# Four attention steps of batches 2 and 3 issued beside the channel mixing of batches 0 and 1, with x allotted at the first product with v

## The chip, the cores and the metric

The kernel runs on one core of one Trainium2 chip. The metric is the device time of an execution in microseconds (us). The profile is one execution of the same program, with its own time.

## What is computed

Three blocks follow each other, for 4 batches of 576 positions with 8 heads of 64 (d_model 512), all in float32. Cut to what matters:

```python
# attention, per batch and head; heads 0-3 see the last 32 positions, heads 4-7 every 4th of the last 128
scores = where(mask, q @ k.T / sqrt(64), -1e9)
x = softmax(scores) @ v                      # heads side by side: (4, 576, 512)
# first mixing block
theta = x @ w_theta
y = w_tok_r @ (x * cos(theta)) + w_tok_i @ (x * sin(theta))   # over positions
u = x + y
x = u + relu(u @ w_ch)                       # over channels
# second block
h = relu(x @ w_in); u, v = halves(h)
out = (u * (w_spatial @ layernorm(v) + b_spatial)) @ w_out
```

## The kernel before

Every float32 product of the mixing blocks is made of three products of rounded parts: a high and a low part of each operand (names ending in _h and _l, zh and zl, uh and ul), high by high, low by high, high by low. The parts are made by `split`: the high part by a cast on ACT, DVE or POOL, the low part by a subtraction on POOL.

The work of a batch b has four stages. `attention(b)` is a generator of 16 steps over 12 groups of rows (four pairs of heads, three groups in each). At a step, `att_values` of the group four steps back, `att_transpose` of the group two steps back and `att_scores` of a new group are issued. Scores are six small products into the PSUM tile s; then, for the batches from 1 on, DVE adds the mask (sm), takes the maximum (m), ACT makes three exponentials with their sums (l), DVE adds a small number and inverts l, and POOL multiplies sm by it. att_transpose turns sm on PE (pt) and copies it to pT. att_values multiplies pT with v (ps_x) and ACT copies the product into x, the batch's activations.

`th_run(b)` runs units of the theta stage, one for each 128 positions: DVE splits x into xh and xl, PE makes ps_th, ACT and DVE reduce it to an angle (ta, tb), ACT takes sine and cosine, PE turns x (ps_xn), DVE multiplies, and the result is split into zh and zl: unit t gives tiles t (cosine) and 4+t (sine), tile 8 holds the last 64 positions of both. `tm_run(b)` mixes positions: 8 units, each one PSUM sum ps_y over all z tiles (27 products with tile 8, 24 without), added to x, then split into uh and ul. `ch_run(b)` mixes channels: 8 units of 12 products (ps_r), added to x, split into a tile "parts" and stored by SP in x2d.

The weights of the second block are split while the first block runs, in 32 jobs (`second`): SP loads a piece, POOL or ACT and DVE turn its 64-bit form into w64g (or it comes as `stage`), a cast and a POOL subtraction fill a tile parts, SP stores it. `parts` has two buffers, which these jobs and the channel mixing share. The PSUM pool ps_mm has four banks, for s, ps_th, ps_y and ps_r. x has two buffers.

`spread(main, (fill, rate), ...)` issues a main generator and, after each of its steps, so many steps of the fills. Batch 0's attention and theta stage come first. Then for b = 0 and 1: tm_run(b) and four units of ch_run(b), with attention(b+1) spread in at two steps a unit; th_run(b+1); and the last four units of ch_run(b). After that come tm_run(2) with attention(3) at three steps a unit (and, chained behind it, one theta unit that batches 2 and 3 share, from the tile xs), then th_run(3) with the rest of batch 2. The second block follows.

That is the order in which the program is issued. A scheduler then places the instructions in one in-order queue for each engine: earlier issued work comes first, and later work goes ahead of it where the scheduler's own times say that the earlier isn't ready. All DMAs go through SP's queue. The text calls the stretch between th_run(1) and tm_run(1) seam A, the same between batches 1 and 2 seam B, and the end of attention(3) with the following xs the tail.

Of the kernel before, what the change touches and what calls it, by code (L numbers as in the profile page):

```python
# [11 lines left out]
F32 = mybir.dt.float32  # L12
# [11 lines left out]
P = 128  # L24
# [19 lines left out]
ATT_RATE, ATT_RATE_PAIR = 2.0, 3.0  # L44
TAIL_RATE = 1.0
CH_BEFORE = 4
PE_MASK = 1
PAIR = 2

# [12 lines left out]
def tile_block(ctx: ExitStack, tc: tile.TileContext, qT, kT, vw, eye_in, mask_in, eye_b_in, w_theta, w_tok, w_ch, w_in, w_sp, w_sph, b_sp, w_out, out):  # L62
# [106 lines left out]
    x = {}  # L169
# [30 lines left out]
    def att_scores(m):  # L200

        b, hp, g = groups[m]
        if g == 0:
            att_load(b, hp)
        if hp == 0 and g == 0:
            x[b] = p1.tile([P, 4, S], F32, tag="x", name=f"x{b}", bufs=2)
        qz, kt, vt, pT = heads[b, hp]
        s = ps_mm.tile([P, 512], F32, tag="mm", name="s")
        kind = 2 * (hp // 2) + g // 2
# [41 lines left out]
    def att_values(m):  # L251

        b, hp, g = groups[m]
        if g == 0:
            return
        qz, kt, vt, pT = heads[b, hp]
        ps = ps_t.tile([P, 512], F32, tag="pt", name="ps_x")
        if g == 1:
            for t in range(NA):
                for j in range(2):  # L260
                    PE.matmul(ps[T * j:T * (j + 1), T * t:T * (t + 1)], vt[:, t, T * j:T * (j + 1)], pT[j][:, T * t:T * (t + 1)], start=True, stop=True)
        else:
            for t in range(NB):
                for j in range(2):
                    PE.matmul(ps[T * j:T * (j + 1), T * t:T * (t + 1)], vt[:, NA + t, T * j:T * (j + 1)], pT[2][:, P * t + T * j:P * t + T * (j + 1)], start=True, stop=True)
        n0, n1 = (0, NA * T) if g == 1 else (NA * T, S)
        if hp < 2:
            A.copy(x[b][:, hp, n0:n1], ps[:, :n1 - n0])
            return

        xv = x[b][:, hp, :].rearrange("p (i r) -> p r i", r=4)
        if g == 1:
            A.copy(xv[:, :2, :], ps[:, :2 * SEQ].rearrange("p (r i) -> p r i", r=2))
            A.copy(xv[:, 2, :NA * T - 2 * SEQ], ps[:, 2 * SEQ:NA * T])
        else:
            A.copy(xv[:, 2, NA * T - 2 * SEQ:], ps[:, :3 * SEQ - NA * T])
            A.copy(xv[:, 3, :], ps[:, 3 * SEQ - NA * T:NB * T])
# [81 lines left out]
    def th_run(b, ts):  # L359
        for t in ts:  # L360
            th_unit(b, t)
            yield
# [46 lines left out]
    def spread(main, *fills):  # L409

        acc = [0.0] * len(fills)
        for _ in main:
            for i, (gen, rate) in enumerate(fills):
                acc[i] += rate
                while acc[i] >= 1.0:
                    acc[i] -= 1.0
                    next(gen, None)
        for gen, _ in fills:
            run(gen)

    def jobs(fns):
        for f in fns:
            f()
            yield

    def take(gen, n):
        for _ in range(n):
            yield next(gen)

    def chain(*gens):  # L430
        for g in gens:
            yield from g
# [11 lines left out]
    second = jobs(j_in + j_sp + j_out)  # L444
    spread(attention(0), (jobs(j_theta + j_tok0), W_RATE0))
    spread(th_run(0, (4, 0, 1, 2, 3)), (jobs(j_tok1), 1.0))
    for b in range(PAIR):
        ch = ch_run(b)
        spread(chain(tm_run(b, K_ALL), take(ch, CH_BEFORE)), (attention(b + 1), ATT_RATE), (take(second, 12) if b else jobs(j_ch), 1.0 if b else 0.5))
        run(th_run(b + 1, (4, 0, 1, 2, 3) if b + 1 < PAIR else (0, 1, 2, 3)))  # L450
        run(ch)


    th_keep(PAIR)
    spread(tm_run(PAIR, K_MAIN, False), (chain(attention(PAIR + 1), th_shared(PAIR)), ATT_RATE_PAIR), (take(second, 10), 1.25))
    spread(th_run(PAIR + 1, (0, 1, 2, 3)), (chain(tm_run(PAIR, (8,)), ch_run(PAIR)), TAIL_RATE), (second, 2.5))
    patt.release()
    ps_v.release()
# [294 lines left out]
```

## Time and profile before

| | before |
|---|---|
| time, three runs | 575.29, 578.91 and 1181.34 us, median 578.91 |
| the profiled execution's own time | 575.99 us |
| its span | 574.2 us |
| mean granted PE clock | 0.973 |
| PE busy | 538.3 us, 94% of the span |
| DVE, POOL, ACT busy | 329.7, 259.6, 243.3 us |

The span is the time between the first and the last record of the profile, which lies within the execution's own time. The granted clock is a share of the full 2.4 GHz. A busy share is a mean over the whole span, and stages differ.

### The profile page before, as it was taken

How to read it: one execution, taken by the hardware profiler on the slowest of the kernel's cores; microseconds unless marked ns; L12 is line 12 of the kernel's file. 1: busy time of each engine (PE TensorE's matmuls, PEld its weight loads, DVE VectorE, ACT ScalarE, POOL GpSimd, SP SyncE). 2: the span in 40 equal slices, each digit the busy share in tenths (PEclk: the TensorE clock that was granted, in tenths of full speed). 3: DMA queues.
4: the chain of work that ended last, by engine and by line, in shares of the span. 5: the costliest groups of instructions: out<-in, count | busy, mean ns of one | idle time of the engine just before them, and what ended most of it. 6: DMA issues, size and time to landing. Idle time of an engine off the chain costs nothing.

```text
span 574.2 us, 11260 instructions
## 1 busy us (share of the span) xinstructions
PE 538.3 (94%) x4148; PEld 479.7 (84%) x4148; DVE 329.7 (57%) x842; ACT 243.3 (42%) x712; POOL 259.6 (45%) x329
## 2 busy tenths in 40 slices
PE   4958889999999999999799999999999999999997
PEld 2745668888988798888688999899889989988996
DVE  3767999965888548956688215773620227354030
ACT  3765475644465624677365111442332223233222
POOL 2755577633696436955339633343211303432040
PEclk9877989999999999999799999999999999999999
DMA  8996224762157644486510699805024120001002
GB/s 226 232 254 176 75 88 113 208 190 83 43 158 231 180 121 153 144 261 211 186 31 1 217 374 373 287 13 166 0 75 132 52 74 1 0 2 57 18 1 92
DMA packets 49935, 76.07 MB, mean 132 GB/s; under 512 B 4052, under 2 KB 30552, under 8 KB 49880
## 3 DMA queue, kind: packets, MB, share of 16 engines
q1 hardware_dynamic: 49880, 75.35, 42.9%
q8 instruction: 33, 0.54, 0.4%
q14 instruction: 22, 0.18, 0.1%
HBM read 52.53 MB, written 22.81 MB: 131 GB/s over the span
## 4 chain that ended last, share of the span: by engine, by line
PE 60%; DVE 13%; DMA 12%; POOL 5%; issue 4%; ACT 3%; SPq 1%; POOLq 0%; ACTq 0%; DVEq 0%
PE ps_y L377 10%; PE ps_sp L628 9%; PE ps_hu L609 9%; PE ps_o L657 9%; PE ps_hv L564 9%; PE ps_r L395 6%; DMA w<-w_tok 3%; PE s L220 2%; DMA w<-w_in 2%; DMA wsp_d<-parts 2%; PE ps_th L322 2%; POOL zl L297 2%; PE pt L247 1%; DMA qz<-qT 1%; DMA w<-w_ch 1%
## 5 line engine op out<-in xcount | busy, mean ns | idle before, releaser
L377 PE MATMUL ps_y<-wtok_h,zh 128*128 128x288 f32 x288 | 87.1, 308 | 3.3 <-DVE sm L231 1.3
L377 PE MATMUL ps_y<-wtok_h,zl 128*128 128x288 f32 x288 | 86.8, 303 | 2.4 <-POOL zl L297 2.4
L377 PE MATMUL ps_y<-wtok_l,zh 128*128 128x288 f32 x288 | 85.3, 297 | 0.0
L377 PEld LDWEIGHTS ps_y<-wtok_h,zh 128*128 128x128 f32 x288 | 53.9, 190 | 7.3 <-DVE sm L231 2.0
L297 POOL TENSOR_TENSOR gl<-hu,gh 128x288 fp32r<-128x288 f32 x32 | 26.0, 813 | 74.4 <-ACT gh L108 74.4
L377 PEld LDWEIGHTS ps_y<-wtok_h,zl 128*128 128x128 f32 x288 | 54.8, 190 | 4.4 <-POOL zl L297 3.2
L377 PEld LDWEIGHTS ps_y<-wtok_l,zh 128*128 128x128 f32 x288 | 54.7, 190 | 0.0
L632 DVE TENSOR_TENSOR hu<-ps_sp,hu 128x288 f32<-128x288 f32 x32 | 14.6, 456 | 67.0 <-PE ps_sp L631 66.9
L297 POOL TENSOR_TENSOR vl<-hv,vh 128x512 fp32r<-128x512 f32 x16 | 20.9, 1309 | 62.7 <-ACT vh L108 57.6
L235 ACT ACTIVATE sm<-sm,m 128x96 f32<-128x96 f32 x108 | 39.2, 364 | 14.6 <-DVE m L232 13.2
L220 PE MATMUL s<-kt,qz 128*64 128x96 f32 x576 | 42.3, 270 | 1.3 <-DMA qz<-qT 0.5
L220 PEld LDWEIGHTS s<-kt,qz 128*64 128x64 f32 x576 | 31.2, 147 | 11.1 <-issue 6.4
L238 POOL TENSOR_TENSOR sm<-sm,l 128x288 f32<-128x288 f32 x48 | 32.1, 673 | 18.1 <-DVE l L237 15.1
L297 POOL TENSOR_TENSOR ul<-x,uh 128x288 fp32r<-128x288 f32 x32 | 26.3, 830 | 27.3 <-ACT uh L108 27.2
L380 DVE TENSOR_TENSOR x<-ps_y,x 128x288 f32<-128x288 f32 x40 | 17.7, 449 | 35.5 <-PE ps_y L377 35.5
L395 PE MATMUL ps_r<-uh,wch_h 128*128 128x288 f32 x128 | 37.8, 296 | 0.0
L628 PE MATMUL ps_sp<-wsp_h,vh 128*128 128x288 f32 x128 | 37.8, 295 | 0.0
L297 POOL TENSOR_TENSOR parts<-x,parts 128x288 fp32r<-128x288 f32 x32 | 26.4, 831 | 25.3 <-ACT parts L108 25.3
L628 PE MATMUL ps_sp<-wsp_l,vh 128*128 128x288 f32 x128 | 37.8, 295 | 0.0
L628 PE MATMUL ps_sp<-wsp_h,vl 128*128 128x288 f32 x128 | 37.8, 295 | 0.0
L609 PE MATMUL ps_hu<-x2h,win_h 128*128 128x288 f32 x128 | 37.7, 294 | 0.0
L609 PE MATMUL ps_hu<-x2h,win_l 128*128 128x288 f32 x128 | 37.7, 294 | 0.0
(157 smaller groups left out, 1589.0 us busy)
## 6 DMA issues: line engine op xcount, KB each, us to landing
x2d<-parts SPq DMA_DIRECT2D x32, 288.0 KB, 2.4
vt<-vw SPq DMA_DIRECT2D x16, 432.0 KB, 4.5
w<-w_tok SPq DMA_DIRECT2D x18, 288.0 KB, 3.2
qz<-qT SPq DMA_DIRECT2D x32, 144.0 KB, 4.3
x2h<-x2d SPq DMA_DIRECT2D x8, 576.0 KB, 7.3
x2l<-x2d SPq DMA_DIRECT2D x8, 576.0 KB, 10.5
kt<-kT SPq DMA_DIRECT2D x15, 304.0 KB, 4.6
w<-w_in SPq DMA_DIRECT2D x16, 256.0 KB, 3.7
```

Source lines behind the costliest of these rows:

```text
L220: PE.matmul(o, qz[:, j, T * t:T * (t + 1)], kt[:, T * t:T * t + KW], start=not on_pe, stop=not on_pe)
L235: A.activation(sm[:, t, :], src[:, t, :], AF.Exp, bias=m_[:, t:t + 1], scale=scale, accum_out=l[:, t:t + 1])
L238: G.tensor_tensor(sm, sm, l.unsqueeze(2).to_broadcast([P, 3, KW]), op=ALU.mult)
L297: (G if el == "g" else V).tensor_tensor(dst_l, src, f32(dst_h), op=ALU.subtract)
L377: PE.matmul(ps[:, :CH], lh[b, k][:, P * d:P * (d + 1)], rh[:, k, cs], start=(n == 0), stop=(n == 3 * len(ks) - 1))
L380: V.tensor_tensor(xv, ps[:, :CH], xv, op=ALU.add)
L395: PE.matmul(ps[:, :CH], lh[:, k, P * e:P * (e + 1)], rh[:, k, cs], start=(n == 0), stop=(n == 11))
L564: PE.matmul(ps, lh[:, k, ts_], rh[:, k, DM:], start=(n == 0), stop=(n == 11))
L609: PE.matmul(ps[:, :CH], lh[:, k, fs], rh[:, k, cs], start=(n == 0), stop=(n == 11))
L628: PE.matmul(ps[:, :CH], lh[b, k][:, fs], rh[:, k, cs], start=(n == 0), stop=False)
L632: V.tensor_tensor(t[:, f, cs], ps[:, :CH], t[:, f, cs], op=ALU.mult)
L657: PE.matmul(ps, lh[:, k, ts_], rh[:, k, cs], start=(n == 0), stop=(n == 11))
```

## The change

Attention of batch b+2 is now made as a generator ahead of the last four units of ch_run(b), and its first four steps are issued one after each of these units. tm_run(b+1) then gets the remaining twelve steps. As no product with v is among the first four steps, the tile x of that batch is allotted in att_values, when the first product is made, instead of at the first scores.

```diff
--- before.py
+++ after.py
@@ -44,6 +44,7 @@
 ATT_RATE, ATT_RATE_PAIR = 2.0, 3.0
 TAIL_RATE = 1.0
 CH_BEFORE = 4
+AHEAD = 4
 PE_MASK = 1
 PAIR = 2
 
@@ -202,8 +203,6 @@
         b, hp, g = groups[m]
         if g == 0:
             att_load(b, hp)
-        if hp == 0 and g == 0:
-            x[b] = p1.tile([P, 4, S], F32, tag="x", name=f"x{b}", bufs=2)
         qz, kt, vt, pT = heads[b, hp]
         s = ps_mm.tile([P, 512], F32, tag="mm", name="s")
         kind = 2 * (hp // 2) + g // 2
@@ -254,6 +253,8 @@
         if g == 0:
             return
         qz, kt, vt, pT = heads[b, hp]
+        if b not in x:
+            x[b] = p1.tile([P, 4, S], F32, tag="x", name=f"x{b}", bufs=2)
         ps = ps_t.tile([P, 512], F32, tag="pt", name="ps_x")
         if g == 1:
             for t in range(NA):
@@ -444,15 +445,18 @@
     second = jobs(j_in + j_sp + j_out)
     spread(attention(0), (jobs(j_theta + j_tok0), W_RATE0))
     spread(th_run(0, (4, 0, 1, 2, 3)), (jobs(j_tok1), 1.0))
+    att_next = attention(1)
     for b in range(PAIR):
         ch = ch_run(b)
-        spread(chain(tm_run(b, K_ALL), take(ch, CH_BEFORE)), (attention(b + 1), ATT_RATE), (take(second, 12) if b else jobs(j_ch), 1.0 if b else 0.5))
+        spread(chain(tm_run(b, K_ALL), take(ch, CH_BEFORE)), (att_next, ATT_RATE), (take(second, 12) if b else jobs(j_ch), 1.0 if b else 0.5))
         run(th_run(b + 1, (4, 0, 1, 2, 3) if b + 1 < PAIR else (0, 1, 2, 3)))
-        run(ch)
+
+        att_next = attention(b + 2)
+        spread(ch, (take(att_next, AHEAD), 1.0))
 
 
     th_keep(PAIR)
-    spread(tm_run(PAIR, K_MAIN, False), (chain(attention(PAIR + 1), th_shared(PAIR)), ATT_RATE_PAIR), (take(second, 10), 1.25))
+    spread(tm_run(PAIR, K_MAIN, False), (chain(att_next, th_shared(PAIR)), ATT_RATE_PAIR), (take(second, 10), 1.25))
     spread(th_run(PAIR + 1, (0, 1, 2, 3)), (chain(tm_run(PAIR, (8,)), ch_run(PAIR)), TAIL_RATE), (second, 2.5))
     patt.release()
     ps_v.release()
```

Three places show how the instructions move in the engines' queues (the number behind a name tells buffers apart; line numbers behind the first edit differ by one or so).

PE's queue at seam A before, where the fifth unit of ch_run(0) ends and the sixth begins (ps_r_1958 and ps_r_1976; ps_xn a theta unit's transposes):

```order
L395 MATMUL ps_r_1958<-ul_968,wch_h_80 128x288
L395 MATMUL ps_r_1976<-uh_967,wch_h_80 128x288
...
L330 MATMUL ps_xn_1940<-ident_63,x1_1006 128x128 x4
L395 MATMUL ps_r_1976<-uh_967,wch_l_81 128x288
L395 MATMUL ps_r_1976<-ul_968,wch_h_80 128x288
```

The same place of PE's queue now (s_1982 and s_2018 are scores of batch 2):

```order
L396 MATMUL ps_r_1958<-ul_968,wch_h_80 128x288
L219 MATMUL s_1982<-kt_1976,qz0_102 64x96 x5
L331 MATMUL ps_xn_1940<-ident_63,x1_1200 128x128 x4
L219 MATMUL s_1982<-kt_1976,qz0_102 64x96
L396 MATMUL ps_r_2000<-uh_967,wch_h_80 128x288
...
L219 MATMUL s_2018<-kt_1976,qz0_102 64x96 x6
```

After each of the last four units of ch_run(0) stands one group of scores; before, scores began only among the ps_y of tm_run(1).

ACT's queue at seam A before, from the reduction of theta unit 2 on (ta_1897 and tb_1898 are unit 2's angles, ta_1936 and tb_1937 unit 3's):

```order
L326 ACTIVATE ta_1897<-ps_th_1884,magic_65 128x512
L108 CAST parts_1990<-x0_118 128x288
L332 ACTIVATE ta_1897<-ta_1897 128x512
L333 ACTIVATE tb_1898<-tb_1898,half_pi_64 128x512
L326 ACTIVATE ta_1936<-ps_th_1923,magic_65 128x512
L108 CAST parts_2008<-x0_118 128x288
L108 CAST parts_2026<-x0_118 128x288
L332 ACTIVATE ta_1936<-ta_1936 128x512
L333 ACTIVATE tb_1937<-tb_1937,half_pi_64 128x512
L235 ACT_TABLE_LOAD
L235 ACTIVATE sm_2077,l_2079<-sm_2077,m_2078 128x96 x3
```

ACT's queue at seam A now, from unit 2's cosine on:

```order
L334 ACTIVATE tb_1898<-tb_1898,half_pi_64 128x512
L234 ACT_TABLE_LOAD
L234 ACTIVATE sm_2025,l_2027<-sm_2025,m_2026 128x96 x2
L327 ACTIVATE ta_1936<-ps_th_1923,magic_65 128x512
L234 ACTIVATE sm_2025,l_2027<-sm_2025,m_2026 128x96
L109 CAST parts_2050<-x0_296 128x288
L248 COPY pT_2058<-pt_2054 96x384
L234 ACTIVATE sm_2067,l_2069<-sm_2067,m_2068 128x96 x3
L109 CAST parts_2092<-x0_296 128x288
L333 ACT_TABLE_LOAD
L333 ACTIVATE ta_1936<-ta_1936 128x512
L334 ACTIVATE tb_1937<-tb_1937,half_pi_64 128x512
```

Exponentials of two groups and two table loads now stand between the sines of unit 2 and unit 3; ahead of unit 2's sine stand one group of exponentials and two loads in the same way, and at seam B one group and two loads ahead of unit 3's.

ACT's queue in the tail before, down to the last copy into x3 (w64g_4055 and the like are pieces of w_out, parts_3973 and the like the casts of such pieces):

```order
L108 CAST parts_3962<-w64g_3965 128x256
L276 COPY x3_3151<-ps_x_3659 128x48
L277 COPY x3_3151<-ps_x_3659 128x144
L249 COPY pT_3672<-pt_3668 96x384
L127 ACTIVATE w64g_4055<-w64_4053 128x256
L108 CAST parts_3973<-w64g_3976 128x256
L249 COPY pT_3678<-pt_3674 96x384
L127 ACTIVATE w64g_4112<-w64_4110 128x256
L108 CAST parts_3984<-w64g_3987 128x256
L273 COPY x3_3151<-ps_x_3680 128x2x144
...
L277 COPY x3_3151<-ps_x_3727 128x144
```

ACT's queue in the tail now:

```order
L278 COPY x3_3265<-ps_x_3579 128x144
L248 COPY pT_3592<-pt_3588 96x384
L248 COPY pT_3635<-pt_3631 96x384
L109 CAST parts_3962<-w64g_3965 128x256
L128 ACTIVATE w64g_4044<-w64_4042 128x256
L274 COPY x3_3265<-ps_x_3637 128x2x144
L275 COPY x3_3265<-ps_x_3637 128x96
L128 ACTIVATE w64g_4055<-w64_4053 128x256
L277 COPY x3_3265<-ps_x_3652 128x48
L278 COPY x3_3265<-ps_x_3652 128x144
L109 CAST parts_3973<-w64g_3976 128x256
```

The last copies into x3 stood behind three casts of w_out pieces and now stand behind one.

## Rows read from the trace of the kernel before

**Rows 1.** Page, part 1: busy us (share), records of each engine.

```profile
PE 538.3 (94%) x4148; PEld 479.7 (84%) x4148; DVE 329.7 (57%) x842; ACT 243.3 (42%) x712; POOL 259.6 (45%) x329
```

**Rows 2.** Windows: length, busy us of five engines (records), PE clock, DMA share, GB/s.

```profile
140.00:160.00 20.00, 20.00 (x140) 17.99 (x139) 15.36 (x28) 9.71 (x18) 12.55 (x13) 1.00 0.13 45
220.00:240.00 20.00, 19.05 (x146) 17.12 (x145) 18.33 (x36) 10.72 (x18) 17.27 (x19) 1.00 0.37 123
```

**Rows 3.** PE timeline, waits between 160 and 310 us: start, us, operation [idle before].

```profile
165.46 0.40 PE L377 MATMUL ps_y<-wtok_h,zh 128*128 128x288 f32 x1 [0.48 <-DVE sm L231]
...
187.96 0.53 PE L247 MATMUL pt<-ident,sm 128*96 128x128 f32 x3 [1.66 <-POOL sm L238]
...
238.42 0.40 PE L377 MATMUL ps_y<-wtok_h,zh 128*128 128x288 f32 x1 [0.54 <-DVE sm L231]
...
307.01 0.40 PE L377 MATMUL ps_y<-wtok_h,zh 128*128 128x288 f32 x1 [0.90 <-DVE ta L327]
```

**Rows 4.** ACT timeline at seam A, 153 to 162 us.

```profile
153.06 0.43 ACT L108 CAST parts<-x 128x288 fp32r<-128x288 f32 x1 [1.12 <-DVE x L398]
...
155.32 0.69 ACT L326 ACTIVATE ta<-ps_th,magic 128x512 f32<-128x512 f32 x1 [0.68 <-POOL zl L297]
156.37 0.43 ACT L108 CAST parts<-x 128x288 fp32r<-128x288 f32 x1 [0.35 <-DVE x L398]
158.38 0.43 ACT L108 CAST parts<-x 128x288 fp32r<-128x288 f32 x1 [1.58 <-DMA x2d<-parts]
158.72 0.63 ACT L332 ACTIVATE ta<-ta 128x512 f32<-128x512 f32 x1
...
159.98 1.28 ACT L235 ACT_TABLE_LOAD   x1
161.27 0.38 ACT L235 ACTIVATE sm<-sm,m 128x96 f32<-128x96 f32 x1
```

**Rows 5.** ACT timeline at seam B: the sine of unit 3.

```profile
235.43 0.63 ACT L332 ACTIVATE ta<-ta 128x512 f32<-128x512 f32 x1 [2.05 <-DVE tb L331]
```

**Rows 6.** Groups by line, ACT: count, busy us, mean ns, idle before.

```profile
L235 ACT ACTIVATE sm<-sm,m 128x96 f32<-128x96 f32 x108 | 39.2, 364 | 14.6 <-DVE m L232 13.2 <-DVE l L237 1.2
...
L235 ACT ACT_TABLE_LOAD x4 | 5.1, 1283 | 0.1
```

**Rows 7.** POOL timeline: last zl of batch 1, and ahead of PE's 1.66 us.

```profile
166.43 1.34 POOL L297 TENSOR_TENSOR zl<-ta,zh 128x512 fp32r<-128x512 f32 x1
...
186.86 0.41 POOL L129 TENSOR_SCALAR w64g<-w 128x256 f32<-128x256 f32 x1 [1.67 <-DVE l L237]
```

**Rows 8.** Windows of the tail.

```profile
272.30:278.40 6.10, 1.96 (x40) 1.56 (x41) 3.94 (x11) 3.71 (x12) 1.67 (x3) 0.77 0.68 225
278.40:282.40 4.00, 4.00 (x18) 3.90 (x19) 3.97 (x8) 1.31 (x4) 1.84 (x3) 0.50 0.44 150
```

**Rows 9.** PE timeline of the tail.

```profile
272.33 0.51 PE L247 MATMUL pt<-ident,sm 128*96 128x128 f32 x3 [0.29 <-DVE pT L249]
...
275.16 0.57 PE L265 MATMUL ps_x<-pT,vt 96*64 96x64 f32 x12 [1.48 <-ACT pT L249]
278.37 1.08 PE L330 MATMUL ps_xn<-ident,xs 128*128 128x128 f32 x4 [2.63 <-DVE xs L310]
```

**Rows 10.** ACT timeline of the tail.

```profile
274.33 0.40 ACT L108 CAST parts<-w64g 128x256 fp32r<-128x256 f32 x1 [1.35 <-DMA wsp_d<-parts]
274.64 0.47 ACT L249 COPY pT<-pt 96x384 f32<-96x384 f32 x1
...
276.41 0.40 ACT L108 CAST parts<-w64g 128x256 fp32r<-128x256 f32 x1 [0.35 <-DMA wo_d<-parts]
```

**Rows 11.** DVE timeline of the tail: xs.

```profile
277.93 0.29 DVE L310 COPY xs<-x 128x256 f32<-128x256 f32 x1 [0.88 <-ACT x L277]
```

**Rows 12.** Chain of waits, 190 to 195 us: start, us, what.

```profile
190.26 3.79 PE ps_y L377 x27
194.05 0.65 PE s L220 x12
```

## The prediction

> **What bounds the kernel now.** I read the page's busy shares first. PE is busy for 94% of the span [rows 1], so the change can only give back time in which PE waits, or works at the lower clock, near the places that it touches. It can't make any product shorter. The PE timeline from 110 to 310 us therefore came next: the idle times in its last column are the whole of what is to be had. Around the seam between batch 0 and batch 1 (call it seam A) PE waits 0.48 us for DVE's mask step. In the attention of batch 2 it waits 1.66 us once for a POOL multiply, and at the end of the last theta stage 0.90 us [rows 3]. Around seam B (batch 1 to batch 2) the stage from 220 to 240 us has PE at 19.05 of 20, so 0.95 us idle [rows 2]; 0.54 of it stands before one ps_y [rows 3]. The largest place is the tail of batch 3's attention: from 272.3 to 278.4 PE is busy for 1.96 of 6.10 us, so 4.14 idle, and from 278.4 to 282.4, after that mostly idle stretch, the granted clock is 0.50, the 1.2 GHz level [rows 8]. Four microseconds at half speed do what two would do, so 2.0 us go there. All together 0.48 + 1.66 + 0.95 + 4.14 + 2.0 + 0.90 = 10.1 us: even if all of it came back, that is 1.8%.
>
> The second thing to see is what the work is moved into. In the stage from 220 to 240 us DVE is busy 18.33 and POOL 17.27 of 20 [rows 2]. The theta units and channel mixing leave these two engines little room, while PE has its own work anyway. Moved scores put mask, maximum and two small operations on DVE, three exponentials on ACT and a multiply on POOL into that stage.
>
> **The change part by part.** *The scores that move.* Four steps of batch 2 go beside the last four ch_run units of batch 0, and four of batch 3 beside those of batch 1. PE, DVE and POOL issue as many operations as before in all, so nothing is removed or added there, only moved; a step's scores cost PE 0.65 us for 12 records [rows 12], wherever they stand. The loads of these steps (first two heads) already stand ahead of the seam in SP's queue before; only the third head's kt and qz move up, past two or three x2d stores. At seam A the DMA engines are busy 13% [rows 2], so I cost the loads at nothing. If the stores came late, a later ACT cast of parts would wait, as one does 1.58 us [rows 4].
>
> *x allotted later.* x has two buffers, and the first product with v comes after the last split of the old x in either order. Nothing waits for it: zero.
>
> *Table loads.* This is the only operation added. ACT needs the Exp table for scores and the Sin table for theta. Scores now stand between the sines of units 1, 2 and 3, so the order has six more ACT_TABLE_LOADs, four at seam A and two at B, of 1.28 us each [rows 6], 7.7 us of ACT. At A the sine of unit 2 gets in front of it one load, three exponentials and the load back: 1.28 + 3 x 0.364 + 1.28 = 3.65 us [rows 6]. ACT had been idle for 1.12 us just ahead [rows 4], so the sine is 2.5 us later. The sine of unit 3 gets two more loads and six exponentials, 2.57 + 2.18 = 4.75, less the idle 0.68 + 0.35 + 1.58 = 2.61 [rows 4]: 2.5 + 4.75 - 2.61 = 4.6 us later than 158.72. What hangs on it is the multiply and cast on DVE and the last zl on POOL, which starts at 166.43 before [rows 7], and without that zl no ps_y group can close. PE has other work meanwhile, three steps of scores that came later before and the first transposes; but it also reaches this zl with fewer ps_y behind it. So the cost lies between 0 (covered) and 4.6 (uncovered). I take 2.2, about the middle.
>
> At seam B only unit 3's sine is cut off: two loads and three exponentials, 3.65, less 2.05 idle ahead of that sine [rows 5], so 1.6 us late, in a stage where DVE and POOL have no slack to make it up. Between 0 and 3.65; I take 1.7, next to the 1.6.
>
> The Trainium skill speaks against this part (ScalarE: Activation LUTs, section What ACT_TABLE_LOAD costs): it puts a switch at 1283 ns for the load and some 1380 ns for a drain, 2.66 us together, and the page's rules say to do all of one set before switching. The trace agrees with the load's length but not with the drain: the load starts at 159.98 and the next ACTIVATE at 161.27 [rows 4]. By the page's sum each load would be 1.38 dearer, unit 3's sine 5.5 us later still at A and 2.8 at B.
>
> *The wait of 1.66 us in batch 2's attention.* There POOL's multiply stood behind a weight conversion that started at 186.86 [rows 7]. The conversions are still strewn between the multiplies in the new POOL order, so the wait may go or move: between -1.66 and 0, I take -0.8.
>
> *The tail of batch 3's attention.* With four steps done ahead, 13 steps at three a unit are left instead of 17, so the attention ends one ps_y unit earlier and that unit (24 products, 24 x 3.79/27 = 3.4 us [rows 12]) comes after it. What held the tail before was ACT: its pT copy stood behind a cast that waited 1.35 us for a store, and the last x copies behind another that waited 0.35 [rows 10]; only then came xs on DVE at 277.93 [rows 11] and PE's transposes of it at 278.37 after 2.63 idle, with 1.48 idle before the last ps_x [rows 9]. The new ACT order has one cast of w_out ahead of the last x copies instead of three. Two casts at the 2.08 us between 274.33 and 276.41 [rows 10] are 4.2 us, so xs comes 4.2 earlier while PE arrives 3.4 earlier: the idle time shrinks by only 0.8. The unit put behind fills the 0.90 wait at 307.01 [rows 3], -0.9. The clock may still fall, as the idle stretch remains over 3 us: between -2.0 and 0, I take -1.0. Sum of the tail -2.7; at best -0.8 - 0.9 - 2.0 and the two store waits of 1.70 as well, -5.4; at worst 0, if the chain of stores arrives no earlier.
>
> *The sum.* +2.2 + 1.7 - 0.8 - 2.7 = +0.4 us on the profiled execution's own 575.99 (span 574.2 and 1.8 around it): 576.4. The undisturbed runs shown are 575.29 and 578.91, the median of the three being the latter, 578.91; the profiled one lies 0.5% below it, and I predict on the profiled one.
>
> **The rivals.** *The tail goes and nothing is paid (569 us).* If other work covers the late sines at both seams, the 1.66 goes, and the tail gives its best (store waits gone, the clock kept at 2.4 GHz, the last wait filled): -1.66 - 5.4 = -7.1, 568.9. For it: PE has 94% of work to hide things behind, and at seam A it waited only 0.48. Against: DVE and POOL are full at seam B, and the ACT tail still has casts that wait for stores.
>
> *The table loads are paid in full (585 us).* ACT alternates between Exp and Sin, the z tiles of units 2 and 3 come late and PE meets them uncovered: +4.6 and +3.65 with nothing back, 584.2. It decides itself at the first ps_y that needs unit 3's zl: if PE stands there more than the forecast's 2.2 us, this case has begun. For it: in-order queues, and PE now meets these tiles with fewer ps_y in front. Against: PE before had other work at the same place and rarely waited. This is also what the Trainium skill's rule on grouping activations by table (ScalarE: Activation LUTs, Rules for kernel authors) would let one expect; with its drain added the time would be 592.5.
>
> That the change moves nothing can be left out: in the order, scores stand between ps_r products.
>
> **How the numbers follow.** The forecast of 576.4 gets 0.55, the first rival 0.22, the second 0.18, and 0.05 is for what I don't see. The range, 568.5 to 583.5, takes in the first rival's 568.9 and nearly reaches the second's 584.2; the run-to-run spread of 3.6 us lies inside. About 2%, 11.5 us, is what a measurement of this kernel can tell from no change. Faster by that would need more than all 10.1 us of waits: 0.03. Slower by that needs the second rival with more on top: 0.05. Within: 0.92.
>
> **What would show it.** In the changed kernel: 11 + 6 table loads. At seam A, PE idle of 2 to 3 us on ps_y with zl as releaser, at about 163 to 171 us. At seam B, 2 to 3 us around 236 to 243. In the tail, xs 3 to 5 us earlier, PE idle of about 3 us ahead of it, and the granted clock either at 0.5 again or not. The theta stage after it should have no 0.90 wait. I am wrong if PE is idle more than 5 us at a seam, or if the tail's idle time is gone altogether, or if a new wait appears where I have none, such as POOL's multiplies queued between the zl of the seam.

## The result and the profile after

The changed kernel takes 582.03 us (median of six runs, 580.86 to 584.02) against 577.07 us before: ratio 1.0100 with an interval of 1.0063 to 1.0137. One of the six runs before took 1181.34 us; it is left out of the ratio, as single slow runs are in the table below. A second series gave 582.74 us, 1.0081 (1.0050 to 1.0111). So the change costs about 5 us, within 2%, where the forecast was 576.4 us, +0.4 on the profiled 575.99. The profiled execution took 581.34 us, with a span of 579.6.

Part 1 of the page after, beside [rows 1]; ACT has 11 records (six of them table loads, five taken over from DVE) and 8 us more, PE 2.5 us more for the same products:

```profile
PE 540.8 (93%) x4148; PEld 481.5 (83%) x4148; DVE 327.9 (57%) x837; ACT 251.4 (43%) x723; POOL 258.9 (45%) x329
```

The two stretches of [rows 2] in the windows after:

```profile
140.00:160.00 20.00, 20.00 (x153) 17.29 (x151) 15.61 (x31) 14.37 (x30) 10.82 (x12) 1.00 0.19 61
220.00:240.00 20.00, 17.86 (x140) 15.42 (x139) 18.78 (x37) 11.76 (x22) 14.17 (x16) 1.00 0.43 138
```

PE is still full at seam A, but ACT went from 9.71 to 14.37 of 20. At seam B PE is idle for 2.14 instead of 0.95.

The table loads are there as counted, six more. The groups by line after show the seven of the scores' line and eight of the sine's, at the length and beside the exponentials of [rows 6]:

```profile
L234 ACT ACTIVATE sm<-sm,m 128x96 f32<-128x96 f32 x108 | 39.3, 365 | 12.5 <-DVE m L231 9.0 <-POOL sm L237 3.1
...
L333 ACT ACT_TABLE_LOAD x8 | 10.3, 1283 | 0.1
L234 ACT ACT_TABLE_LOAD x7 | 9.0, 1283 | 0.1
```

PE's waits after, from its timeline, beside [rows 3] and [rows 9]:

```profile
163.37 0.40 PE L378 MATMUL ps_y<-wtok_h,zl 128*128 128x288 f32 x1 [0.29 <-POOL zl L298]
168.27 0.69 PE L262 MATMUL ps_x<-pT,vt 96*64 96x64 f32 x16 [0.26 <-ACT pT L248]
189.42 0.53 PE L246 MATMUL pt<-ident,sm 128*96 128x128 f32 x3 [1.85 <-POOL sm L237]
232.05 0.40 PE L396 MATMUL ps_r<-uh,wch_h 128*128 128x288 f32 x1 [2.14 <-DVE ta L328]
...
266.74 0.88 PE L246 MATMUL pt<-ident,sm 128*96 128x128 f32 x6 [1.27 <-ACT x L269]
275.92 1.48 PE L246 MATMUL pt<-ident,sm 128*96 128x128 f32 x6 [2.79 <-issue]
280.86 0.63 PE L331 MATMUL ps_xn<-ident,xs 128*128 128x128 f32 x4 [1.37 <-DVE xs L311]
...
311.01 0.40 PE L378 MATMUL ps_y<-wtok_h,zh 128*128 128x288 f32 x1 [1.89 <-DVE ta L328]
312.88 0.37 PE L396 MATMUL ps_r<-uh,wch_h 128*128 128x288 f32 x1 [0.41 <-DVE x L381]
```

The late zl of seam A costs 0.29, far less than the 2.2 forecast there. The wait for POOL's multiply stayed (1.85), the tail's waits sum to 1.27 + 2.79 + 1.37 = 5.43 (before 4.86, of it 4.40 in [rows 9]), and the 0.90 at the end of the theta stage became 1.89 + 0.41.

To see where the time goes, the program is best cut at work that both kernels have: from the first ps_r of seam A to the first ps_th of batch 2, from there to the transposes of xs, from there to the first ps_r of batch 2. The windows of the kernel before, cut so:

```profile
145.65:213.35 67.70, 65.55 (x652) 59.52 (x651) 46.97 (x122) 34.44 (x119) 41.48 (x55) 1.00 0.50 148
213.35:278.37 65.02, 59.21 (x583) 51.73 (x581) 48.20 (x124) 40.11 (x132) 41.68 (x52) 0.98 0.61 196
278.37:307.51 29.14, 28.25 (x153) 24.95 (x153) 23.10 (x43) 12.92 (x25) 14.06 (x15) 0.93 0.21 65
```

And those of the kernel after:

```profile
144.68:214.70 70.02, 67.51 (x652) 61.29 (x651) 46.39 (x122) 39.03 (x124) 41.10 (x55) 0.98 0.49 145
214.70:280.86 66.16, 57.94 (x558) 49.73 (x557) 46.81 (x112) 42.27 (x134) 40.17 (x51) 0.97 0.58 178
280.86:312.88 32.02, 29.44 (x176) 26.11 (x177) 25.80 (x50) 14.64 (x28) 16.89 (x18) 1.00 0.27 86
```

Call them stretches 1, 2 and 3. The lengths add up to 161.86 and 168.20, +6.3 us: PE's idle time (length less busy) rose from 8.85 to 13.31, the rest is busy time, all of it in stretch 1, where the clock is lower. 24 products, the ps_y unit put behind, moved from stretch 2 to 3 (581 weight loads against 557); stretch 2 did not get shorter for it, stretch 3 got longer by 2.9.

The lower clock in stretch 1 shows in two short windows after, right behind the wait for sm:

```profile
186.00:190.00 4.00, 2.04 (x34) 1.65 (x33) 2.99 (x10) 0.81 (x2) 2.15 (x5) 1.00 1.00 298
190.00:195.00 5.00, 5.00 (x28) 4.84 (x27) 2.91 (x11) 3.33 (x15) 1.85 (x3) 0.66 0.93 264
```

PE works half of the first and all of the second, at a granted 0.66 on the mean, which lies between 0.5, the 1.2 GHz level, and 1; before, the whole stretch has 1.00, and 27 ps_y took 3.79 us [rows 12].

### The profile page after: what moved, and what is told of

Its sections match the earlier page's. It is cut to its first block, busy times and chain, and to the rows that moved or that the text cites. A ratio compares the mean times of both kernels' runs of the same rounds, so it can differ in the third digit from the quotient of the medians.

```text
span 579.6 us, 11270 instructions
## 1 busy us (share of the span) xinstructions
PE 540.8 (93%) x4148; PEld 481.5 (83%) x4148; DVE 327.9 (57%) x837; ACT 251.4 (43%) x723; POOL 258.9 (45%) x329
## 3 DMA queue, kind: packets, MB, share of 16 engines
q1 hardware_dynamic: 49880, 75.35, 42.9%
## 4 chain that ended last, share of the span: by engine, by line
PE 46%; DVE 4%; DMA 4%; POOL 2%; ACT 2%; issue 2%; SPq 0%; POOLq 0%; ACTq 0%; DVEq 0%
PE ps_sp L632 9%; PE ps_hu L613 9%; PE ps_o L661 9%; PE ps_hv L568 9%; PE ps_y L378 5%; PE ps_r L396 4%; DMA wsp_d<-parts 2%; DMA wo_d<-parts 1%; POOL parts L144 1%; DMA win_d<-parts 1%; PE ps_sp L635 1%; PE ps_sp L634 1%; DVE ta L328 1%; ACT parts L109 0%; DVE tb L332 0%
## 5 line engine op out<-in xcount | busy, mean ns | idle before, releaser
L298 POOL TENSOR_TENSOR ul<-x,uh 128x288 fp32r<-128x288 f32 x32 | 25.9, 815 | 42.9 <-ACT uh L109 41.9
L219 PE MATMUL s<-kt,qz 128*64 128x96 f32 x576 | 40.7, 265 | 3.2 <-DMA qz<-qT 2.3
L237 POOL TENSOR_TENSOR sm<-sm,l 128x288 f32<-128x288 f32 x48 | 32.1, 673 | 13.7 <-DVE l L236 11.7
L396 PE MATMUL ps_r<-uh,wch_l 128*128 128x288 f32 x128 | 37.7, 295 | 0.0
L613 PE MATMUL ps_hu<-x2l,win_h 128*128 128x288 f32 x128 | 37.7, 295 | 0.0
```

Of the source, the lines that this page charges most:

```text
L219: PE.matmul(o, qz[:, j, T * t:T * (t + 1)], kt[:, T * t:T * t + KW], start=not on_pe, stop=not on_pe)
L237: G.tensor_tensor(sm, sm, l.unsqueeze(2).to_broadcast([P, 3, KW]), op=ALU.mult)
L298: (G if el == "g" else V).tensor_tensor(dst_l, src, f32(dst_h), op=ALU.subtract)
L396: PE.matmul(ps[:, :CH], lh[:, k, P * e:P * (e + 1)], rh[:, k, cs], start=(n == 0), stop=(n == 11))
L613: PE.matmul(ps[:, :CH], lh[:, k, fs], rh[:, k, cs], start=(n == 0), stop=(n == 11))
```

## The experiments

My first theory after this comparison, **Q**, was that queues and PSUM banks make the loss at and behind the second seam, where DVE and POOL are full, and that the table loads hide. Its rival, **L**, was that the added table loads make it. **S** is that casts which wait for stores hold ACT's queue. "The whole change" is the kernel after; ratios are to the kernel before, timed with them; 0.1% is 0.58 us.

| run | what | median us | ratio (interval) |
|---|---|---|---|
| e1 | ahead at seam A alone | 579.42 | 1.0033 (1.0006, 1.0059) |
| e2 | ahead at seam B alone | 580.11 | 1.0038 (1.0012, 1.0065) |
| e3 | the four steps behind the mixing | 579.70 | 1.0037 (1.0013, 1.0061) |
| e4 | the whole change, slower spread | 582.05 | 1.0065 (1.0037, 1.0092) |
| e5 | before, no sine table | 576.27 | 0.9983 (0.9963, 1.0003) |
| e6 | the whole change, no sine table | 577.12 | 0.9990 (0.9967, 1.0013) |
| e7 | before, three parts | 579.95 | 1.0061 (1.0041, 1.0081) |
| e8 | the whole change, three parts | 580.30 | 1.0052 (1.0030, 1.0074) |
| e9 | the whole change, six loads out | 577.72 | 0.9994 (0.9974, 1.0015) |
| e10 | the whole change again | 582.74 | 1.0081 (1.0050, 1.0111) |
| e11 | before, the unit moved alone | 578.78 | 1.0014 (0.9988, 1.0040) |
| e12 | steps behind, slower spread | 575.00 | 0.9941 (0.9919, 0.9964) |
| e13 | loads of seam A out | 579.56 | 1.0050 (1.0029, 1.0072) |
| e14 | loads of seam B out | 579.71 | 1.0054 (1.0025, 1.0082) |
| e15 | six loads out, slower spread | 576.98 | 0.9995 (0.9971, 1.0019) |
| e16 | steps behind at seam A alone | 577.07 | 0.9996 (0.9973, 1.0020) |

**e1 and e2, one seam at a time.**

```diff
-        spread(ch, (take(att_next, AHEAD), 1.0))
+        spread(ch, (take(att_next, 0 if b else AHEAD), 1.0))      # e1
+        spread(ch, (take(att_next, AHEAD if b else 0), 1.0))      # e2
```

> Four steps ahead at the seam between batches 0 and 1 only; the second seam and the tail are as in the kernel before. The order of ACT has 4 of the 6 added table loads. Theory Q (the loss is made by queues and PSUM banks where DVE and POOL are full, which is at the second seam and behind it): the last products of batch 2's theta stage came 1.35 us late in the whole change, and seam A is all that lies ahead of them, so +1.4 us (0 to 2.3) over the kernel before. Theory L (each added table load costs its share of the +5.0): 4/6 of 5.0, +3.3 us.

> Four steps ahead at the seam between batches 1 and 2 only; 2 of the 6 added table loads. Theory Q: the rest of the loss, 5.4 - 1.4, so +3.5 to +4 us over the kernel before, with the wait of about 2 us on a ps_r at the seam, zl late by some 6 us, and a theta stage of batch 3 that is 2 to 3 us longer. Theory L: 2/6 of 5.0, +1.7 us.

Each costs about 2 us, 1.9 and 2.2, and together they nearly make the whole. That is between the theories (1.4 and 3.5 by Q, 3.3 and 1.7 by L) and decides nothing. One thing in e2's profile mattered later: its program up to seam B is that of the kernel before, and yet stretch 1 takes 70.01 us there, with a wait of 2.57 for POOL's multiply and a fall of the granted clock, against 67.70 in the profile that the prediction read.

**e3, the steps behind the mixing and not between its units.**

```diff
-        spread(ch, (take(att_next, AHEAD), 1.0))
+        run(ch)
+        run(take(att_next, AHEAD))
```

> The four steps are issued behind the last unit of the channel mixing and not between its units, at both seams. ACT's order then has 11 table loads as before, none added. Theory L: no loss, 577 us, within 1 us of the kernel before. Theory Q: what is lost behind the seams stays (the tail's store waits, the theta stage with a ps_y unit ahead of its products, together about 2 us) and what is lost in the seams goes (about 2 to 3 us), so +1.5 to +3 us.

11 loads and still +2.1 us: as Q had it. Stretch 1 is 66.16 us here; stretch 3 with the moved unit is 35.05.

**e4, the slower spread of attention(3).**

```diff
-ATT_RATE, ATT_RATE_PAIR = 2.0, 3.0
+ATT_RATE, ATT_RATE_PAIR = 2.0, 2.25
```

> The whole change, with attention(3) spread at 2.25 steps a unit of tm_run(2) instead of 3, so that the 13 steps that are left end at the sixth unit again as the 17 did before, and no ps_y unit more than before stands behind it. Theory Q with the moved unit as a cost of its own: the theta stage of batch 3 from xs to the first ps_r of batch 2 is back at about 29.6 us (32.5 in the whole change), 2 to 3 us faster than the whole change, +2.5 over the kernel before. If that unit costs nothing by itself (theory L, or a longer theta stage for another reason): +5, as the whole change.

Stretch 3 went back to 30.07 us as expected, but stretch 2 grew to 68.67, and the time is within the spread of the whole change. Putting the unit back ahead gained nothing clear of noise here.

**e5 and e6, no sine table.** In both kernels sine and cosine are replaced by exponentials, which leaves out the right values.

```diff
-        A.activation(ta, ta, AF.Sin, scale=-TURN)
-        A.activation(tb, tb, AF.Sin, scale=-TURN, bias=half_pi[:n, 0:1])
+        A.activation(ta, ta, AF.Exp, scale=-TURN)
+        A.activation(tb, tb, AF.Exp, scale=-TURN, bias=half_pi[:n, 0:1])
```

> The kernel before with the sine and the cosine of the theta stage replaced by exponentials of the same operands, which leaves out the right values of z and with them the output; the queues of all engines hold the same instructions in the same order, but ACT has 2 table loads and not 11. Theory L (table loads on the path): each of the 9 that go would give back up to 1.28 us, and the kernel gets faster by several us. Theory Q (they lie under other work): within 1 us of the kernel before.

> The same replacement in the whole change, so the output is left out of account again; ACT has 2 table loads and not 17, everything else in the order of the whole change. Theory L: it takes as long as the kernel before without tables (difference 0 to 1 us), since the six loads are all that the change adds. Theory Q: the difference of the two stays at +4 to +5 us, since the order of ACT's casts and sines is that of the whole change.

Theory Q, as the account of the whole loss, fell here. The nine loads that go from the kernel before give back 1.0 us in all (between 2.1 gained and 0.2 lost); the fifteen that go from the whole change give back about 5, and the two kernels are then 0.07% apart by their ratios. The +2.1 of e3, without a load added, is not explained by L.

**e7 and e8, three buffers of parts.**

```diff
-tag="parts", name="parts", bufs=2)
+tag="parts", name="parts", bufs=3)
...
-                pool, n_ = (const, 2) if b < B - 1 else (p2s, 8)
+                pool, n_ = (const, 3) if b < B - 1 else (p2s, 8)
```

> The kernel before with three buffers of parts instead of two, so that an ACT cast of parts waits less for the store of an earlier one. Theory S (casts that wait for stores stand in ACT's queue ahead of theta's and attention's operations): the waits of 1.35 and 0.35 us in the tail of batch 3's attention go, and the kernel is 1 to 2 us faster than the kernel before. Theory L: no change.

> The whole change with three buffers of parts. Theory S: ACT's waits of 3.2 us for a store ahead of the first theta unit at the second seam and of 3.05 and 1.57 us in the tail go, so it is 2 to 4 us faster than the whole change and at most 2 us slower than the kernel before with three buffers; ta is then not late at the second seam and the 2.1 us wait of ps_r goes. Theory L: it stays 5 us above the kernel before with three buffers.

The pair differs by -0.1%, as S would have it, but this can't be used for S: the scheduler placed the instructions anew (more than 90 of some 840 DVE rows stand elsewhere in either kernel), and the kernel before got 3.5 us slower, where S expected it faster. Inconclusive.

**e9, the six added loads out and nothing else.** With Exp in three theta units, every engine holds the instructions of the whole change in its order, less six ACT_TABLE_LOADs.

```diff
+        fn = AF.Exp if (b, t) in ((1, 2), (1, 3), (2, 3)) else AF.Sin
-        A.activation(ta, ta, AF.Sin, scale=-TURN)
-        A.activation(tb, tb, AF.Sin, scale=-TURN, bias=half_pi[:n, 0:1])
+        A.activation(ta, ta, fn, scale=-TURN)
+        A.activation(tb, tb, fn, scale=-TURN, bias=half_pi[:n, 0:1])
```

> The whole change with sine and cosine replaced by exponentials in units 2 and 3 of the theta stage of batch 1 and unit 3 of batch 2 alone, which leaves out the right values there. Each engine has the instructions of the whole change in its order, less exactly the six added table loads (17 become 11). Theory L, by the pair without tables (they differ by 0.8 us): within 1 to 1.5 us of the kernel before, 4 us faster than the whole change. Theory Q: 1 us or less faster than the whole change, and what the pair without tables gave back came from loads that the kernel before has as well.

**e10, the whole change again**, on the same chip as e9:

> The whole change, unchanged, beside the others on the same chip. All theories: 4 to 5.5 us over the kernel before (ratio 1.007 to 1.010). Its second profile tells which waits recur: by theory L the late sines (zl at the first seam, the ps_r at the second, the mask step behind them), by theory Q those of the tail and of batch 3's theta stage.

577.72 against 582.74: the six loads cost 5.0 us, some 2 us either way by the intervals, and that is all of the loss. No run changes the values alone, but e5, with other values in every theta unit and nine loads fewer, moved by 1.0 us only. In e9 the windows of the three stretches are

```profile
146.10:212.20 66.10, 65.32 (x652) 59.68 (x651) 45.69 (x122) 34.10 (x120) 41.36 (x55) 1.00 0.51 152
212.20:276.39 64.19, 57.03 (x558) 49.37 (x557) 47.18 (x112) 39.59 (x132) 40.51 (x51) 0.97 0.59 184
276.39:309.59 33.20, 30.87 (x176) 27.58 (x177) 26.16 (x50) 14.70 (x28) 16.58 (x18) 0.95 0.27 84
```

and in e10

```profile
145.58:215.82 70.24, 67.59 (x653) 61.13 (x651) 46.87 (x122) 39.13 (x124) 41.20 (x55) 0.98 0.48 144
215.82:282.27 66.45, 58.78 (x558) 50.95 (x557) 46.87 (x112) 42.51 (x134) 40.22 (x50) 0.92 0.58 177
282.27:315.51 33.24, 30.94 (x176) 27.82 (x177) 26.14 (x50) 14.70 (x28) 16.80 (x18) 0.94 0.26 83
```

The profiles recur: 70.0 and 70.2 in stretch 1 with the four loads of seam A, 66.1 without. (The other three kernels with these loads have 70.38, 69.64 and 68.16: e1, e4, e14.) How they get onto the path is seen on ACT. Its timeline after at seam A, beside [rows 4]:

```profile
150.95 1.28 ACT L234 ACT_TABLE_LOAD   x1
152.25 0.38 ACT L234 ACTIVATE sm<-sm,m 128x96 f32<-128x96 f32 x1
...
153.78 1.28 ACT L333 ACT_TABLE_LOAD   x1
155.07 0.64 ACT L333 ACTIVATE ta<-ta 128x512 f32<-128x512 f32 x1
155.61 0.71 ACT L334 ACTIVATE tb<-tb,half_pi 128x512 f32<-128x512 f32 x1
156.33 1.28 ACT L234 ACT_TABLE_LOAD   x1
...
161.74 1.28 ACT L333 ACT_TABLE_LOAD   x1
163.04 0.63 ACT L333 ACTIVATE ta<-ta 128x512 f32<-128x512 f32 x1
163.57 0.71 ACT L334 ACTIVATE tb<-tb,half_pi 128x512 f32<-128x512 f32 x1
164.30 1.28 ACT L234 ACT_TABLE_LOAD   x1
...
167.76 0.46 ACT L248 COPY pT<-pt 96x384 f32<-96x384 f32 x1
```

From 150.25 on ACT hardly idles until 169.7. Twelve us of it, the window from the first ps_r + 12, after:

```profile
156.68:168.68 12.00, 11.45 (x121) 9.89 (x121) 11.29 (x26) 11.79 (x37) 9.45 (x12) 1.00 0.62 182
```

and in e9, at the same place:

```profile
158.10:170.10 12.00, 12.00 (x132) 10.68 (x130) 11.90 (x32) 7.40 (x31) 12.00 (x15) 1.00 0.65 200
```

ACT is busy for 11.79 of 12 with the loads, 7.40 without: it has become the fullest engine there, and POOL, which is full without them, is busy for 9.45. PE has passed 121 of its records there, not 132. What PE meets late is the zl (0.29) and then the pT copy that ACT reaches at 167.76 (0.26), and it stays behind to the wait for sm: 1.85 at 189.42, of which e9 has

```profile
188.43 0.53 PE L246 MATMUL pt<-ident,sm 128*96 128x128 f32 x3 [0.78 <-POOL sm L237]
...
229.82 0.40 PE L397 MATMUL ps_r<-uh,wch_h 128*128 128x288 f32 x1 [2.41 <-DVE ta L328]
```

only 0.78, and no fall of the clock after it. POOL's multiply waits there for the l of DVE, and that stands in DVE's queue behind a cast of w_in that waits for a store. The rows after (DVE's cast, POOL's multiply), beside [rows 7]:

```profile
187.01 0.29 DVE L111 CAST parts<-w64g 128x256 fp32r<-128x256 f32 x1 [1.72 <-DMA win_d<-parts]
...
188.70 0.67 POOL L237 TENSOR_TENSOR sm<-sm,l 128x288 f32<-128x288 f32 x1 [0.59 <-DVE l L236]
```

and DVE's in e9:

```profile
186.01 0.29 DVE L111 CAST parts<-w64g 128x256 fp32r<-128x256 f32 x1 [1.52 <-DMA win_d<-parts]
```

Counted from the first ps_r of the seam this cast is at 42.3 us after and at 39.9 in e9, 2.4 later, while PE comes to the wait only 1.3 later (187.57 and 187.65, so 42.9 and 41.6): the weight jobs, whose operations stand in the same queues as the seam's, lost more than PE did. Which of them first, I did not follow. Of the 3.9 us by which stretch 1 is longer than in e9, 1.3 are this arrival, 1.1 the longer wait, and 1.7 the clock behind it (5 us at 0.66); the three come to 0.2 more than the whole.

The second line of e9's PE rows shows that the wait at seam B is no work of the loads: it is 2.41 without them. It is there in part when seam A alone is changed (1.21 in e1, 1.09 in e16) and not when seam B alone is (e2).

**e11, the moved unit alone**, in the kernel before.

```diff
-ATT_RATE, ATT_RATE_PAIR = 2.0, 3.0
+ATT_RATE, ATT_RATE_PAIR = 2.0, 3.5
```

> The kernel before with attention(3) spread at 3.5 steps a unit instead of 3, so that it ends one ps_y unit earlier, as in the whole change, and this unit stands in the theta stage of batch 3; nothing ahead, no table load more. If the moved unit has a price by itself: idle time of some 2.5 us in that stage (0.9 in the kernel before) and 1.5 us over the kernel before, with the tail's idle time as before. If it fills waits, as the prediction had it: 0 to 1 us faster.

+0.8 us, with an interval that includes zero. Stretch 3 is 31.39, 2.3 longer for 24 products of 3.4 us, so the 0.90 wait was filled in part (0.30 + 0.41 are left); stretches 2 and 3 together are 95.22 against 94.16. No gain of the unit shows.

**e12, steps behind the mixing and the slower spread**: the edits of e3 and e4 together.

> Steps behind the channel mixing (11 table loads, as before) and attention(3) at 2.25 steps a unit, so that neither the table loads nor the moved unit are there. If these two are the loss: 0 to 1 us from the kernel before, or faster by what the filled waits give (up to 1.7 us); 2 us faster than the kernel with the steps behind alone. If not, +2 us as that kernel.

The fastest of all, 0.6% under the kernel before, with an interval (0.9919 to 0.9964) that lies below 1 as a whole; its windows are

```profile
145.36:211.34 65.98, 65.71 (x652) 59.80 (x651) 45.48 (x125) 32.83 (x117) 41.66 (x55) 1.00 0.50 152
211.34:276.60 65.26, 59.63 (x582) 51.82 (x581) 47.29 (x116) 40.00 (x132) 41.25 (x51) 1.00 0.63 191
276.60:305.92 29.32, 28.07 (x153) 24.57 (x153) 24.20 (x46) 14.08 (x27) 14.58 (x16) 0.94 0.24 76
```

Idle time is 7.15 us instead of 8.85. Stretch 1 is 1.7 shorter than before, and stretches 2 and 3, which lose 3.2 in e9, are as long as before (94.58 against 94.16).

**e13 and e14, the loads of one seam out.**

```diff
+        fn = AF.Exp if (b, t) in ((1, 2), (1, 3)) else AF.Sin      # e13
+        fn = AF.Exp if (b, t) in ((2, 3),) else AF.Sin             # e14
```

> The whole change with the exponentials in place of sine and cosine in units 2 and 3 of batch 1's theta stage alone (right values left out there): the four table loads added at the first seam are gone, the two at the second stay. If the first seam pays most (the two profiles of the whole change take 70.0 and 70.2 us from the first ps_r there to batch 2's theta products, the two without its loads 66.1): 3.5 to 4 us faster than the whole change, about 1 us over the kernel before. If the loads pay alike: 3.3 us faster. If the second seam pays most: 1.5 us or less.

> The whole change with the exponentials in unit 3 of batch 2's theta stage alone (right values left out there): the two table loads added at the second seam are gone, four at the first stay. If the first seam pays most: 1 to 1.5 us faster than the whole change, 3.5 to 4 us over the kernel before. If the loads pay alike: 1.7 us faster. If the second seam pays most: 3.5 us or more.

Against the two series of the whole change (1.0081 and 1.0100) the four loads of seam A are worth 1.8 to 2.9 us, the two of seam B 1.6 to 2.7: each ratio has an interval of 1.2 to 2.1 us either way, so which seam pays more, in all or per load, is not shown. The profile of e13 has stretch 1 at 65.58, that of e14, which keeps the loads of seam A, at 68.16 with no fall of the clock.

**e15, six loads out and the slower spread**: the edits of e9 and e4 together.

> The six loads out as in the run before that left them out, and attention(3) at 2.25 steps a unit so that the ps_y unit is back ahead of its end. If the unit behind it costs about what the two kernels with the steps behind the channel mixing differ by (5.5 us, of it 3.6 in the profiles of the stages and the rest the clock): 3 to 5 us faster than the six loads out alone, so 574 to 575. If the unit's place is worth 1 us or less, as the whole change with the slower spread let one think: 577.

No gain: 0.9995 against 0.9994. So the slower spread is worth, by the ratios, 5.5 us when the steps stand behind the mixing (e3 against e12), 1 to 2 when they stand between with the loads (e4 against the whole change), and nothing without the loads.

**e16, steps behind at seam A alone.**

```diff
-        spread(ch, (take(att_next, AHEAD), 1.0))
+        run(ch)
+        run(take(att_next, 0 if b else AHEAD))
```

> The four steps behind the last unit of channel mixing at the first seam alone; 11 table loads, the second seam and the tail as in the kernel before. If steps ahead without table loads take away the POOL wait and the fall of the granted clock in batch 2's attention: 66 us from the first ps_r of the seam to batch 2's theta products, where kernels with the order of before have 67.7 to 70.6, and the time is 2.5 to 3.5 us below the kernel before. If that was chance: within 1 us of it.

Stretch 1 is 66.00 us, as expected, and the time is not below that of the kernel before: stretches 2 and 3 are 96.19 together, 2 more than the 94.16 of its profile. Stretch 1 is shorter in every profile with steps ahead and no load added, but by itself that did not make the kernel faster. Nor did the rest stay as before: by the traces the scheduler placed stretches 2 and 3 anew, though the program is changed at seam A alone. Scores of batch 3 stand elsewhere among the ps_y at 235 to 242 us, and ACT has casts of w_sp and copies of pT in another order from 247 us on. e1, which has nearly this order there, takes 96.26 us for the two stretches. So neither run tells what shorter seams would be worth with the old order behind them.

## Why the prediction was wrong

*The seams.* The count of loads was right, and their prices nearly so: 2.2 + 1.7 = 3.9 forecast, 1.8 to 2.9 and 1.6 to 2.7 measured, 5.0 together in one series. The path was not the one argued, so that the prices are near is luck. Seam A was to pay at the last zl, behind a late sine. The sine of unit 3 was late (163.04 against 158.72, and the seam began 1.0 earlier), but PE lost 0.29 at the zl. With the loads ACT is full for 19 us, and PE loses more at the multiply of 1.85 and in the lower clock after it. At seam B the sine of unit 3 was to be 1.6 late; by ACT's timeline after it starts at 239.47, behind a load that follows three exponentials,

```profile
238.18 1.28 ACT L333 ACT_TABLE_LOAD   x1
239.47 0.63 ACT L333 ACTIVATE ta<-ta 128x512 f32<-128x512 f32 x1
```

against 235.43 in [rows 5]: 4.0 later, of which 1.4 is the later start of the whole stage. How the two loads there get onto PE's path the profiles don't show: PE's wait at the seam is 2.14, 2.27 and 2.82 with them (after, e10, e13), 2.41 and 2.49 without (e9, e14), and 0.38 and 0.24 at zl tiles (247.69 and 248.98) stand in one of the three alone. The wait of 2.14 for ta was not forecast; e9 shows that the loads don't make it, and e12 has it at 1.67 and is faster than the kernel before all the same.

*The wait of 1.66 us.* Forecast at -0.8: without the loads it is 0.78, so -0.9, and with them 1.85. Not seen was what hangs on it. Four profiles have the order of the kernel before at that place: the one read, e2, e5 and e11. Stretch 1 is 67.70, 70.01, 70.59 and 70.60 us in them; in the last three the clock fell, in the one read it did not. All seven kernels with steps ahead at seam A and no load added there (e3, e6, e9, e12, e13, e15, e16) have 65.58 to 66.16. So up to 4 us were to be had in this stretch, more than the one profile showed, and the four loads take them back (68.16 to 70.38 in the five profiles that have them). e16 shows no gain in the median: what is won there is lost again behind it, in an order that is no longer that of before.

*The tail: the step that failed.* The sum set this -2.7 (and the wait's -0.8) against the loads; e9, which is the change without the loads, is 0.3 us below the kernel before (between 1.5 below and 0.9 above), not the 3.5 of tail and wait together. Its stretches 2 and 3 are 97.39 us where the kernel before has 94.16: 3.2 longer, not 2.7 shorter. (e5, whose order there is that of before, has 95.65.) By term, against the profile of the kernel before:

| | forecast | in e9 |
|---|---|---|
| waits of the tail | -0.8 | 4.61 for 4.86: -0.25 |
| waits at the end of the theta stage | -0.9 | 2.32 for 0.90: +1.4 |
| PE's busy time, by the clock | -1.0 | 87.90 for 87.46: +0.4 |
| wait at seam B, no load added | none | 2.41 for 0.95: +1.5 |

(4.61 is 0.59 + 2.57 + 1.45; 4.86 is 0.46, at 260.69, and 0.29 + 1.48 + 2.63 of [rows 9].)

"xs comes 4.2 earlier while PE arrives 3.4 earlier" is wrong in both halves. Counted from the start of stretch 2, xs came 64.6 us in before, 63.8 in e9 and 65.7 in the kernel after; PE was ready for its transposes at 62.4, 62.7 and 64.8. The rows of e9, DVE's and PE's:

```profile
275.95 0.29 DVE L311 COPY xs<-x 128x256 f32<-128x256 f32 x1
...
276.39 1.09 PE L331 MATMUL ps_xn<-ident,xs 128*128 128x128 f32 x4 [1.45 <-DVE xs L311]
```

The 3.4 us of products that left stretch 2 were made up by waits, the 2.41 at seam B and the 2.57 ahead of a pt at 271.44, which ends 0.1 after ACT has copied x out of a ps_x (270.96, for 0.37). I had taken the two casts fewer ahead of the x copies at 2.08 each, but casts of w_sp that stand earlier in the queue wait longer for their stores. ACT's timeline of the tail after, beside the 1.35 and 0.35 of [rows 10]:

```profile
264.39 0.43 ACT L109 CAST parts<-stage 128x288 fp32r<-128x288 f32 x1 [3.05 <-DMA wsp_d<-parts]
...
272.07 0.43 ACT L109 CAST parts<-stage 128x288 fp32r<-128x288 f32 x1 [1.57 <-DMA wsp_d<-parts]
273.27 0.43 ACT L109 CAST parts<-stage 128x288 fp32r<-128x288 f32 x1 [0.76 <-DMA wsp_d<-parts]
```

The weight jobs behind these stores begin later: DVE's first cast of w_in in that stage is at 246.81 instead of 240.79, or 32.1 us after the start of stretch 2 instead of 27.4 (31.4 in e9). So the chain of casts and stores that the tail waits for moved back; xs on DVE comes at 280.42,

```profile
280.42 0.29 DVE L311 COPY xs<-x 128x256 f32<-128x256 f32 x1 [0.31 <-ACT x L278]
```

where [rows 11] have 277.93. Why the weight jobs start later stays open. The channel mixing, which shares the two parts buffers with them and now has four groups of scores between its units, suggests itself, but the same cast comes 31.6 us after the start of stretch 2 in e12, with the groups behind the mixing, and 30.9 in e16, with none at that seam; e7 and e8 were to separate it, and did not. The clock term brought nothing that can be counted on: PE's busy time in stretches 2 and 3 is 87.46 before, 87.38 after, 89.72 in e10 and 87.90 in e9. The unit put behind was to fill the 0.90 wait; e9 has 1.90 and 0.42 there, e11 0.30 and 0.41.

*The rivals.* "The table loads are paid in full" (584.2) had the mechanism, loads paid and nothing back, and was the nearer one. Its sign, PE at the zl of unit 3, did not show; it should have been ACT's busy share. Of the same loads the Trainium skill (ScalarE: Activation LUTs, What ACT_TABLE_LOAD costs) would make 2.66 us each by its load and drain, an estimate of 16 for six; the runs have 5.0, less than the 7.7 that the six last by themselves. The Trainium skill's rule to do all of one table set before switching (ScalarE: Activation LUTs, Rules for kernel authors) agrees with e9, which is 5.0 us faster without the six switches. "The tail goes and nothing is paid" is what e12 comes nearest to, with no load added and the unit kept ahead: 3.4 us faster, not 7.

*What is left open.* Why the slower spread is worth 5.5 us in one order and nothing in another, and why the sums of the stretches give e9 and e16 a little more than the medians do: a profile is one execution, and stretches 2 and 3 of the order before differ by 1.5 us between two of them (94.16, and 95.65 in e5). The slower spread, too, makes the scheduler place that part anew, so e12 does not show which of its moves counts.

## What to carry to other kernels

Before moving work into a stage, add up the receiving engine's time there, table loads too: ACT, busy for 9.71 of 20 us, looked free enough, and with four loads and the exponentials it was busy for 11.79 of 12. Keep functions of different tables apart in an engine's queue: the same four steps, issued behind the channel mixing instead of between its units, need no load. That alone was 0.4% slower than the kernel before (e3); with the spread set so that no unit changes sides it is 0.6% faster (e12). Book a gain only where the last thing to arrive has been shown to move: two casts taken out of the tail's queue gave nothing, as others ahead of them waited longer. And where a scheduler places the program, compare the queues behind an edit before laying a difference to it: e16 changes one seam and has another order 80 us behind it.

## What was not expected of the hardware

The price of a table load hangs on its place: six added ones cost 5.0 us, 0.84 each (e9, e10), while nine that go from the kernel before give back 1.0 us together (e5, with zero inside the interval), at the same 1283 ns.

A wait of PE under 2 us can cost more than itself. Behind the 1.85 for POOL's multiply the granted clock is 0.66 over 5 us, which do what 3.3 do at full clock, so another 1.7 us go there. But the length of the wait alone does not tell: at the same place the clock fell behind 1.75 (e1), 2.05 (e11), 2.30 (e5) and 2.57 us (e2), and in e10 behind 0.32 and 1.49, and it stayed at 1.00 behind 0.78 (e9), 1.39 (e14), 1.66 (the kernel before) and 2.19 (e4). Stretch 1 of e14 and of e4, with no fall in it:

```profile
143.89:212.05 68.16, 65.99 (x652) 59.78 (x651) 46.14 (x122) 39.06 (x124) 41.17 (x55) 1.00 0.49 147
146.03:215.67 69.64, 66.22 (x652) 59.78 (x651) 46.68 (x122) 39.21 (x124) 41.14 (x55) 1.00 0.49 145
```
